# Feature projections on half rows of the matrix engine in one burst, four banks read in two orders, and a last output group in two halves

## The chip, the cores and the metric

The kernel runs on one core of a Trainium2 chip. The core has five engines that run side by side, each through its own list of instructions: TensorE (PE in the profile; its weight loads are listed apart as PEld), VectorE (DVE), ScalarE (ACT), GpSimd (POOL) and SyncE (SP, which here only issues transfers). Matmuls write to PSUM, which the kernel uses as eight banks of 128 partitions by 512 fp32 values. The metric is the device time in microseconds (us). Differences below 0.2% are about what a measurement of this kernel can't tell from no change.

## What is computed

Two stages, for batch 8, 8 heads, 576 tokens, head size 64:

```python
def phi(x):                                   # q and k, (8, 8, 576, 64) -> (8, 8, 576, 256)
    proj = einsum('bhsd,df->bhsf', x, w_phi)  # 128 features
    proj = proj - max(abs(proj), axis=-1, keepdims=True)
    return concatenate([exp(proj), exp(-proj)], axis=-1)
kv  = einsum('bhsf,bhsd->bhfd', phi(k), v)
num = einsum('bhsf,bhfd->bhsd', phi(q), kv)
den = einsum('bhsf,bhf->bhs', phi(q), sum(phi(k), axis=2)) + 1e-06
x   = num / den                               # then heads side by side: (8, 576, 512)

h = relu(x @ w_in)                            # (8, 576, 1024)
u, v = h[..., :512], h[..., 512:]
v = (v - mean(v)) / sqrt(var(v) + 1e-06)
v = einsum('ts,bsd->btd', w_spatial, v) + b_spatial[None, :, None]
out = (u * v) @ w_out                         # (8, 576, 512), fp32
```

Note the subtraction of the largest absolute projection. For keys the kernel takes the exponentials without it and scales the values by the exponential of the maximum; for queries it adds the negated maximum inside the matmul that makes the features.

## The kernel before

**Units.** The attention is cut into 36 units. A pair unit is two heads of one batch on 512 of its 576 tokens (four blocks of 128 per head); there are four for each of the eight batches. The remaining 64 tokens of two batches, all eight heads, make one tail unit, so there are four of these. A unit's keys and queries stand in SBUF as `kT` and `qT`: 128 partitions, of which the lower 64 hold the 64 dimensions of one block of tokens and the upper 64 those of another, times four column groups of 128 tokens.

**Projection by token.** `by_token` (L263 to L268) makes half a unit's projections: two matmuls with a column group of `kT` or `qT` as the weights and `wphi2` as the moving operand. `wphi2` is 128 by 256 and block diagonal: `w_phi` in the upper left, `w_phi` in the lower right, zeros elsewhere. So half of the products of each matmul are with zeros. One PSUM bank takes the two results, four blocks of 128 features.

**Readers of the banks.** `a_keys` (L270) does two halves, each: two matmuls, then the maximum on VectorE (`mk`, L278), then two exponentials on ScalarE (`kf`, L281). `a_queries` (L283) does two halves of matmuls and maxima only (`mq`, L292), and then `mhl` splits the maxima into two bf16 parts (L295, L296; GpSimd, or VectorE in the first five units). `a_scale` (L298) makes `em` on ScalarE from `mk`, and GpSimd scales the values with it into `vs` (L306).

**Order of the work.** `step(i)` writes the instructions of one step by hand, in the order of the list `ORDER` (L622). Each entry names a piece of work for a unit, some steps behind by `LAGS`, followed by a share of filler: `fill` pops tasks of the second stage from a queue while a credit lasts. The tasks of a batch come to 16.7 us by the costs that the kernel gives them (`MM` = 0.85 us and `MS` = 1.07 us), over 4.5 units, so a step has about 3.7 us of filler. The tasks are `b_v` (v half of w_in, L447, evicted by ScalarE at L449, statistics on VectorE at L450), `b_u` (L515, L517), `b_s` (spatial matmul L536 and L537, product on VectorE at L539), and `b_o` (output, L561, evicted by VectorE and ScalarE in turn at L564, sent off by SyncE at L570) with their 64-token tails.

**The other pieces of a step.** `sums` is `a_kv` (L378, L380), `attention` is `a_num` (L398, then L388 and L389 on VectorE), `features` is `a_qfeat` (L344, exponentials at L365), `maxima` is `a_max_t` (L327, then L330 and L331 on VectorE), `next` is `a_transpose`, which from batch 2 on has nothing to do for pair units since they are transposed by transfers.

**PSUM.** All PSUM tiles come from one pool of eight banks (`psum`, tag `bank`). A matmul that takes a bank anew waits until all readers of the bank's last tile are done.

**The end.** `out_tasks` (L598) of the last batch are four `b_o` and then `b_o_tail` (L572), which evicts 128 rows and sends them as two transfers of 64 rows each.

Of the kernel before, what the change touches and what calls it, by code (L numbers as in the profile page):

```python
# [8 lines left out]
FP32 = mybir.dt.float32  # L9
BF16 = mybir.dt.bfloat16  # L10
AF = mybir.ActivationFunctionType
ALU = mybir.AluOpType
AX = mybir.AxisListType
# [3 lines left out]
def kernel(  # L17
# [15 lines left out]
    nc = tc.nc  # L33

    B, H, S, D = q.shape
    F = w_phi.shape[1]
    DM = moe_w_in.shape[0]
    DFF = moe_w_in.shape[1]
    HALF = DFF // 2
    P = 128  # L40
    KC = DM // P
    NP = H // 2
    NB = 4
# [3 lines left out]
    POS = [0, 2, 1, 3]  # L47
# [5 lines left out]
    feat = ctx.enter_context(tc.tile_pool(name="feat", bufs=2))  # L53
    small = ctx.enter_context(tc.tile_pool(name="small", bufs=3))
    s2 = ctx.enter_context(tc.tile_pool(name="stage_b", bufs=2))

    psum = ctx.enter_context(tc.tile_pool(name="psum", bufs=8, space=bass.MemoryType.PSUM))
# [13 lines left out]
    st = {}  # L71
# [67 lines left out]
    bias = cpool.tile([P, NB], FP32)  # L139
# [8 lines left out]
    wphi2 = cpool.tile([P, 2 * F], BF16)  # L148
# [10 lines left out]
    NM = 3  # L159
    mhl, mT = [], []  # L160
    for i in range(NM):
        for tiles, name in ((mhl, "mhl"), (mT, "mT")):
            t = cpool.tile([P, P], BF16, name=f"{name}{i}")
# [21 lines left out]
    for y in range(2):  # L185
        r = slice(y * D, (y + 1) * D)
# [7 lines left out]
    for i in range(2):  # L194
        pin(nc.scalar.copy)(out=alternate(wm, i),
                            in_=wphi2[:, i * F:(i + 1) * F].unsqueeze(1).to_broadcast([P, NP, F]))
# [20 lines left out]
    w_out_bf = cpool.tile([P, KC, DM], BF16)  # L217
# [7 lines left out]
    EARLY = 5  # L225
# [22 lines left out]
    def a_transpose(u):  # L248
        if u["pair"] and u["b"] >= XB:
            return  # L250
        src = st[u["b"]] if u["pair"] else gs[u["g"]]
        for x, copy in (("k", nc.vector.tensor_copy if u["i"] < EK else nc.scalar.copy), ("q", nc.vector.tensor_copy)):
            pt = psum.tile([P, 4, P], BF16, tag="bank", name="pt")
            for j in range(4):
                if u["pair"]:
                    blk = src[x][u["pj"] // 2][:, 2 * (u["pj"] % 2) + j // 2, (j % 2) * P:(j % 2 + 1) * P]
                else:
                    blk = src[x][:, 2 * j:2 * j + 2, :]
                nc.tensor.transpose(out=pt[:, j, :], in_=blk, identity=ident)
            u[x + "T"] = a1.tile([P, 4, P], BF16, tag="kT", name="kT") if x == "k" else qts[u["i"] % len(qts)]  # L260
            copy(out=u[x + "T"], in_=pt)

    def by_token(xT, half):  # L263
        ps = psum.tile([P, 4, F], FP32, tag="bank", name="ps")
        for x in range(2):
            nc.tensor.matmul(out=ps[:, 2 * x:2 * x + 2, :], lhsT=xT[:, 2 * half + x, :], rhs=wphi2,  # L266
                             start=True, stop=True)
        return ps  # L268

    def a_keys(u):  # L270

        u["mk"] = small.tile([P, H], FP32, tag="mk", name="mk")
        u["kf"] = feat.tile([P, 2, H, F], BF16, tag="kf" if u["pair"] else "kf_t", name="kf",
                            bufs=4 if u["pair"] else 2)
        for half in range(2):
            pk = by_token(u["kT"], half)
            hs = slice(4 * half, 4 * half + 4)
            nc.vector.tensor_reduce(out=u["mk"][:, hs], in_=pk, axis=AX.X, op=ALU.max,  # L278
                                    apply_absolute_value=True)
            for s, sc in ((0, 1.0), (1, -1.0)):  # L280
                nc.scalar.activation(out=u["kf"][:, s, hs, :], in_=pk, func=AF.Exp, bias=0.0, scale=sc)  # L281

    def a_queries(u):  # L283

        m, early = mhl[u["i"] % NM], u["i"] < EARLY
        if not early:
            mq = small.tile([P, H], FP32, tag="mq", name="mq")
        for half in range(2):
            pq = by_token(u["qT"], half)
            if early and half == 0:  # L290
                mq = pq[:, 0, 0:H]
            nc.vector.tensor_reduce(out=mq[:, 4 * half:4 * half + 4], in_=pq, axis=AX.X, op=ALU.max,  # L292
                                    apply_absolute_value=True)
        eng = nc.vector if early else nc.gpsimd
        eng.tensor_copy(out=m[:, 0:H], in_=mq)  # L295
        eng.tensor_tensor(out=m[:, H:2 * H], in0=mq, in1=m[:, 0:H], op=ALU.subtract)  # L296

    def a_scale(u):  # L298
        em = small.tile([P, 2, H], FP32, tag="em" if u["pair"] else "em_t", name="em", bufs=3 if u["pair"] else 1)
# [25 lines left out]
    def a_max_t(u):  # L325
        pt = psum.tile([P, P], BF16, tag="bank", name="pt")
        nc.tensor.transpose(out=pt, in_=mhl[u["i"] % NM], identity=ident)  # L327
        if merged(u):
            odd, even = u["qT"][0:2 * H], u["qE"][D:D + 2 * H]
            nc.vector.tensor_copy(out=odd, in_=pt[0:2 * H, :].unsqueeze(1).to_broadcast([2 * H, 4, P]))  # L330
            nc.vector.tensor_copy(out=even, in_=pt[0:2 * H, :].unsqueeze(1).to_broadcast([2 * H, 4, P]))  # L331
            return
        nc.vector.tensor_copy(out=mT[u["i"] % NM][0:2 * H, :], in_=pt[0:2 * H, :])
# [224 lines left out]
    def o_mm(lhs, r):  # L558
        po = psum.tile([P, DM], FP32, tag="bank", name="po")
        for dc in range(KC):  # L560
            nc.tensor.matmul(out=po[r], lhsT=lhs(dc), rhs=w_out_bf[:, dc, :], start=(dc == 0), stop=(dc == KC - 1))  # L561
        ob = s2.tile([P, DM], FP32, tag="ob", name="ob", bufs=6)
        turn[0] ^= 1
        (nc.vector.tensor_copy if turn[0] else nc.scalar.copy)(out=ob[r], in_=po[r])  # L564
        return ob

    def b_o(b, j):
        ob = o_mm(lambda dc: st[b]["uT"][:, dc, j * P:(j + 1) * P], slice(0, P))
        dst = bass.AP(tensor=out.tensor, offset=out.offset + b * S * DM + POS[j] * DM, ap=[[NB * DM, P], [1, DM]])
        nc.sync.dma_start(out=dst, in_=ob)  # L570

    def b_o_tail(g, bls):  # L572
        r = slice(bls[0] * TL, (bls[-1] + 1) * TL)
        ob = o_mm(lambda dc: gs[g]["uTt"][:, dc, r], r)
        for bl in bls:
            nc.sync.dma_start(out=out[2 * g + bl, T0:S, :], in_=ob[bl * TL:(bl + 1) * TL, :])
# [18 lines left out]
    MM = KC * T0 / 2400.0  # L595
    MS = (KC + 1) * T0 / 2400.0

    def out_tasks(b):  # L598
        ts = [(MM, lambda j=j: b_o(b, j)) for j in range(NB)]
        if b % 2:  # L600
            ts.append((MM, lambda: b_o_tail(b // 2, [0, 1])))
        return ts

    def b_tasks(b):
# [11 lines left out]
        for y in range(NB):  # L616
# [2 lines left out]
        ts.append((MS / 2, lambda: b_s_tail(g, [bl])))  # L619
        return ts + (out_tasks(b) if b == B - 1 else [])  # L620

    ORDER = (("keys", 0.375), ("queries", 0.25), ("attention", 0), ("sums", 0.25),  # L622
             ("next", 0.125), ("features", 0), ("out", 0), ("maxima", 0))
    MOST = 4.0
    rate = [MOST]
    CAP = 2.11
# [5 lines left out]
    def fill(share):  # L632
        credit[0] = min(credit[0] + rate[0] * share, CAP)
        while queue and credit[0] >= queue[0][0] / 2:
            cost, task = queue.pop(0)
            task()
            credit[0] -= cost
# [3 lines left out]
    def lag(u, what):  # L641
        if u["i"] < 5:
            return (HEAD if u["i"] < 2 else FIRST if u["pair"] else FT).get(what, 0)
        return LAGS.get(what, 0)
# [3 lines left out]
    def step(i):  # L648

        if i == 0:  # L650
            a_transpose(units[0])
        left = [p - i + 1 for p in lists if p >= i]
        rate[0] = min(MOST, sum(cost for cost, _ in queue) / left[0]) if left else MOST
        for what, share in ORDER:
            for u in units[max(0, i - 5):i + 2]:
                if u["i"] + lag(u, what) != i or (what in ("sums", "attention", "out") and not u["pair"]):
                    continue
                last = u["pair"] and u["pj"] == NP - 1
                if what == "keys":
                    a_keys(u)  # L660
                    a_scale(u)
                elif what == "sums":
                    a_kv(u)
                elif what == "queries":
                    a_queries(u)
                elif what == "next":
                    a_transpose(u)
                elif what == "maxima":
                    a_max_t(u)
                elif what == "out":  # L670
                    a_x_t(u)
                    if last:
                        finish_batch(u, tail_x_t)
                        queue.extend(b_tasks(u["b"]))
                elif what == "features":
                    a_qfeat(u)
                elif what == "attention":
                    a_num(u)
                    if last:
                        finish_batch(u, tail_num)  # L680
            fill(share)

    def finish_batch(u, f):
        f(u["g"], [u["b"] % 2])
# [34 lines left out]
    for u in units:  # L719
        i = u["i"]  # L720
# [48 lines left out]
```

## Time and profile before

| | |
|---|---|
| time, median of 3 runs | 278.79 us (278.53 to 278.94) |
| span of the profiled execution | 275.7 us |
| POOL busy | 184.4 us, 67% of the span |
| PEld busy | 171.3 us, 62% |
| granted TensorE clock | full in all 40 slices |
| L281, `kf`, ACT | 144 instructions, 638 ns each, 75.4 us busy |
| L365, `qf`, ACT | 128 instructions, 625 ns each, 66.6 us busy |
| L278, `mk`, DVE | 72 instructions, 681 ns each, 46.3 us busy |
| L292, `mq`, DVE | 62 and 10 instructions, 678 and 690 ns each, 46.8 us busy |
| L266, `ps`, PE | 288 matmuls of 256 columns, 272 to 296 ns each by kind |

The duration of a single instruction includes a tail in which the next one of the same engine already runs: neighbouring matmuls of 256 columns have 273 ns each but start 109 ns apart. So for an engine's rate, starts are read, or the length of a merged run of instructions. Busy time counts overlapping stretches once. The clock is full all the time, so no difference in what follows comes from it.

### The profile page before, as it was taken

The numbers are of one execution on the slowest core, as the hardware profiler recorded it, in microseconds if no ns is written. First come the engines' busy times: TensorE is split into PE (matmuls) and PEld (weight loads), VectorE is DVE, ScalarE is ACT, GpSimd is POOL, SyncE is SP. The second block draws the span as 40 slices with busy tenths as digits, with TensorE's granted clock in tenths as the row PEclk, the third lists the DMA queues.
The fourth block names the chain that finished last, engine by engine and source line by source line (L and its number), as shares of the span: only waits on it lengthen the run. The fifth ranks groups of instructions, "written<-read, shape, count | busy, mean of one in ns | idle before, by whom it ended". The sixth has DMA issues, their size and how long they took to land.

```text
span 275.7 us, 8138 instructions
## 1 busy us (share of the span) xinstructions
PE 254.7 (92%) x3007; PEld 171.3 (62%) x3047; DVE 236.5 (86%) x614; ACT 218.1 (79%) x501; POOL 184.4 (67%) x312
## 2 busy tenths in 40 slices
PE   3778999999999999999998999999998999999993
PEld 2467776777665766666665775766655765554441
DVE  7989999879999889998889899988898897565751
ACT  7898999797698978999798979998798977633511
POOL 7999899999569945897787954997347632410200
PEclk9999999999999999999999999999999999999999
DMA  7999999999999997999999998899744301211115
GB/s 209 230 228 146 164 155 113 181 208 122 202 200 219 232 212 133 232 176 199 156 110 221 258 183 146 171 233 176 104 89 118 88 2 73 81 40 40 76 40 190
DMA packets 84840, 42.43 MB, mean 154 GB/s; under 512 B 51840, under 2 KB 80192, under 8 KB 84800
## 3 DMA queue, kind: packets, MB, share of 16 engines
q1 hardware_dynamic: 60240, 30.95, 54.5%
q0 software_dynamic: 24400, 10.89, 38.5%
q8 instruction: 24, 0.39, 0.6%
q14 instruction: 16, 0.13, 0.2%
q10 hardware_dynamic: 160, 0.07, 0.1%
HBM read 32.85 MB, written 9.44 MB: 153 GB/s over the span
## 4 chain that ended last, share of the span: by engine, by line
PE 70%; ACT 14%; DVE 11%; issue 3%; ACTq 0%; DVEq 0%
PE pv L447 10%; PE ps L536 10%; PE po L561 9%; PE pu L515 8%; PE ps L266 7%; ACT kf L281 7%; PE pv L378 4%; PE pn L398 4%; ACT qf L365 4%; DVE mk L278 3%; PE pq L344 3%; PE ps L537 2%; PE pn L426 2%; ACT vr L449 1%; PE pu L527 1%
## 5 line engine op out<-in xcount | busy, mean ns | idle before, releaser
L306 POOL TENSOR_TENSOR vs<-v_f,em 128x512 bf16<-128x512 f32 x64 | 65.4, 1042 | 27.8 <-ACT em L301 25.3
L281 ACT ACTIVATE kf<-ps 128x512 bf16<-128x512 f32 x144 | 75.4, 638 | 6.5 <-DVE mk L278 6.5
L365 ACT ACTIVATE qf<-pq 128x512 bf16<-128x512 f32 x128 | 66.6, 625 | 9.6 <-PE pq L344 7.5
L278 DVE TENSOR_REDUCE mk<-ps 128x4 f32<-128x512 f32 x72 | 46.3, 681 | 0.7
L292 DVE TENSOR_REDUCE mq<-ps 128x4 f32<-128x512 f32 x62 | 39.9, 678 | 2.2 <-PE ps L266 2.0
L561 PE MATMUL po<-w_out_bf,uT 128*128 128x512 bf16 x120 | 31.9, 379 | 1.4 <-ACT kf L281 0.8
L461 POOL TENSOR_TENSOR rs<-var,neghalf 64x1 f32<-64x1 f32 (+1 forms) x16 | 12.8, 797 | 30.5 <-DVE var L456 30.3
L536 PE MATMUL ps<-w_spT,vn 128*128 128x512 bf16 x119 | 32.5, 379 | 0.5
L450 DVE BATCH_NORM_STATS2 stats<-vr 128x6 f32<-128x512 bf16 (+1 forms) x40 | 26.7, 684 | 6.5 <-ACT vr L449 6.2
L447 PE MATMUL pv<-w_in_bf,xT 128*128 128x512 bf16 x117 | 30.7, 379 | 1.2 <-ACT kf L281 0.6
L515 PE MATMUL pu<-xT,w_in_bf 128*128 128x512 bf16 x119 | 31.1, 379 | 0.5 <-issue 0.2
L449 ACT ACTIVATE vr<-pv 128x512 bf16<-128x512 f32 (+1 forms) x40 | 23.8, 620 | 8.9 <-PE pv L447 8.1
L539 DVE TENSOR_TENSOR uT<-ps,uT 128x512 bf16<-128x512 f32 x32 | 22.0, 687 | 8.5 <-PE ps L537 7.6
L378 PE MATMUL pv<-vs,kf 128*128 128x66 bf16 x512 | 24.5, 193 | 1.3 <-ACT kf L281 1.1
L389 DVE TENSOR_TENSOR x<-pn,rc 128x256 bf16<-128x256 f32 x64 | 25.0, 416 | 0.3
L398 PEld LDWEIGHTS <-qf 128*128 128x128 bf16 x512 | 20.2, 97 | 7.4 <-issue 1.7
L517 ACT ACTIVATE uT<-pu 128x512 bf16<-128x512 f32 x32 | 19.7, 643 | 6.3 <-PE pu L515 3.2
L378 PEld LDWEIGHTS <-kf 128*128 128x128 bf16 x512 | 21.7, 97 | 3.6 <-issue 2.9
L398 PE MATMUL pn<-kv,qf 128*128 128x66 bf16 x512 | 21.9, 193 | 0.9 <-ACT kf L281 0.3
L380 PE MATMUL pv<-vst,kf 128*128 128x66 bf16 x128 | 21.2, 192 | 1.4 <-POOL vst L61 1.4
L564 ACT COPY ob<-po 128x512 f32<-128x512 f32 x18 | 11.0, 613 | 14.3 <-PE po L561 8.8
L467 POOL TENSOR_SCALAR vn<-vr,rs 128x512 bf16<-128x512 bf16 x28 | 21.2, 764 | 0.9
(130 smaller groups left out, 562.6 us busy)
## 6 DMA issues: line engine op xcount, KB each, us to landing
out_dram<-ob SPq DMA_DIRECT2D x32, 256.0 KB, 2.7
v_f<-in_v_dram SPq DMA_DIRECT2D x14, 512.0 KB, 5.6
k_bf<-in_k_dram POOLq DMA_DIRECT2D x14, 256.0 KB, 6.3
q_bf<-in_q_dram POOLq DMA_DIRECT2D x14, 256.0 KB, 5.9
qt<-qT_b SPq DMA_DIRECT2D x24, 64.0 KB, 4.2
v_tl<-in_v_dram SPq DMA_DIRECT2D x8, 128.0 KB, 5.9
v_f<-in_v_dram SPq DMA_DIRECT2D x1, 1024.0 KB, 8.8
w_in_bf<-in_moe_w_in_dram POOLq DMA_DIRECT2D x2, 512.0 KB, 7.0
```

The costliest lines, as they stand in the source:

```text
L278: nc.vector.tensor_reduce(out=u["mk"][:, hs], in_=pk, axis=AX.X, op=ALU.max, apply_absolute_value=True)
L281: nc.scalar.activation(out=u["kf"][:, s, hs, :], in_=pk, func=AF.Exp, bias=0.0, scale=sc)
L292: nc.vector.tensor_reduce(out=mq[:, 4 * half:4 * half + 4], in_=pq, axis=AX.X, op=ALU.max, apply_absolute_value=True)
L306: nc.gpsimd.tensor_tensor(out=vs[:, s, :, 0:D], in0=st[u["b"]]["v"][:, pj * H:(pj + 1) * H, :], in1=em[:, s, :].unsqueeze(2).to_broadcast( ...
L365: nc.scalar.activation(out=qf[:, s], in_=pq, func=AF.Exp, bias=0.0, scale=sc)
L378: nc.tensor.matmul(out=pv[:, hh, s, :], lhsT=u["kf"][:, s, 4 * hh + c, :], rhs=u["vs"][:, s, 4 * hh + c, :], start=(c == 0), stop=False)
L398: nc.tensor.matmul(out=pn[:, pos, :], lhsT=u["qf"][hh][:, s, pos, :], rhs=d["kv"][:, 2 * u["pj"] + hh, s, :], start=(s == 0), stop=(s == 1))
L447: nc.tensor.matmul(out=pv[r], lhsT=lhs(kc), rhs=w_in_bf[:, kc, HALF:DFF], start=(kc == 0), stop=(kc == KC - 1))
L450: nc.vector.bn_stats(out=stats[r], in_=dst[r])
L515: nc.tensor.matmul(out=pu, lhsT=w_in_bf[:, kc, dc * P:(dc + 1) * P], rhs=d["xT"][:, kc, :], start=(kc == 0), stop=(kc == KC - 1))
L536: nc.tensor.matmul(out=ps, lhsT=d["vn"][:, sp, cs], rhs=w_spT[:, sp, 0:T0], start=(sp == 0), stop=False)
L561: nc.tensor.matmul(out=po[r], lhsT=lhs(dc), rhs=w_out_bf[:, dc, :], start=(dc == 0), stop=(dc == KC - 1))
```

## The change

Three edits:

1. `by_token` makes the projections of a whole `kT` or `qT` with eight matmuls of 128 columns that use 64 rows each: block `j` of the lower half with the upper left `w_phi`, into bank 0, then block `j` of the upper half with the lower right `w_phi`, into bank 1. `a_project` does so for keys and queries, one after the other, so four banks are filled in one burst of 16 matmuls.
2. `a_readers` writes the reads. VectorE takes key bank 0, query bank 0, key bank 1, query bank 1. ScalarE takes key bank 1 and then key bank 0. So the first reads of the two engines are of different banks. The places of the results are interleaved to match (`parity`, and the rearranged `hi` and `lo` of `mhl`), and `mhl` now stands ahead of `vs` on GpSimd. `ORDER` loses the entry `queries`; its share of filler, 0.25, goes to the end of the step, behind `maxima`.
3. The last batch's output has its tail as the second of five groups, and the last group of 128 rows is done by `b_o_last` as two halves of 256 columns, one evicted by ScalarE and sent from ScalarE's queue, one evicted by VectorE and sent from SyncE's.

The purpose is to leave out the products with zeros, to let two engines read at once, and to shorten what follows the last matmul.

```diff
-    def by_token(xT, half):
-        ps = psum.tile([P, 4, F], FP32, tag="bank", name="ps")
-        for x in range(2):
-            nc.tensor.matmul(out=ps[:, 2 * x:2 * x + 2, :], lhsT=xT[:, 2 * half + x, :], rhs=wphi2,
-                             start=True, stop=True)
+    def by_token(xT):
+        ps = [psum.tile([P, 4, F], FP32, tag="bank", name="ps") for _ in range(2)]
+        for j in range(4):
+            for y in range(2):
+                r = slice(y * D, (y + 1) * D)
+                nc.tensor.matmul(out=ps[y][:, j, :], lhsT=xT[r, j, :], rhs=wphi2[r, y * F:(y + 1) * F],
+                                 start=True, stop=True)
         return ps
...
+    def a_project(u):
+        u["pk"], u["pq"] = by_token(u["kT"]), by_token(u["qT"])
...
+        def features(y):
             for s, sc in ((0, 1.0), (1, -1.0)):
-                nc.scalar.activation(out=u["kf"][:, s, hs, :], in_=pk, func=AF.Exp, bias=0.0, scale=sc)
...
+                nc.scalar.activation(out=kf[:, s].rearrange("p (j two) f -> p j two f", two=2)[:, :, y, :],
+                                     in_=u["pk"][y], func=AF.Exp, bias=0.0, scale=sc)
+
+        most(parity(mk, 0), u["pk"][0])
+        features(1)
+        most(mq[:, 0:4], u["pq"][0])
+        features(0)
+        most(parity(mk, 1), u["pk"][1])
+        most(mq[:, 4:8], u["pq"][1])
         eng = nc.vector if early else nc.gpsimd
...
+    def b_o_last(b, j):
...
+        for y, copy, queue_ in ((0, nc.scalar.copy, nc.scalar), (1, nc.vector.tensor_copy, nc.sync)):
+            n = slice(y * DM // 2, (y + 1) * DM // 2)
+            po = psum.tile([P, DM // 2], FP32, tag="bank", name="po")
+            for dc in range(KC):
+                nc.tensor.matmul(out=po, lhsT=st[b]["uT"][:, dc, j * P:(j + 1) * P], rhs=w_out_bf[:, dc, n],
+                                 start=(dc == 0), stop=(dc == KC - 1))
+            ob = s2.tile([P, DM], FP32, tag="ob", name="ob", bufs=6)
+            copy(out=ob[:, 0:DM // 2], in_=po)
+            queue_.dma_start(out=dst[:, n], in_=ob[:, 0:DM // 2])
...
+        if b == B - 1:
+            ts = ts[:1] + ts[-1:] + ts[1:NB - 1] + [(MM, lambda: b_o_last(b, NB - 1))]
...
-    ORDER = (("keys", 0.375), ("queries", 0.25), ("attention", 0), ("sums", 0.25),
-             ("next", 0.125), ("features", 0), ("out", 0), ("maxima", 0))
+    ORDER = (("keys", 0.375), ("attention", 0), ("sums", 0.25),
+             ("next", 0.125), ("features", 0), ("out", 0), ("maxima", 0.25))
...
                 if what == "keys":
-                    a_keys(u)
+                    a_project(u)
+                    a_readers(u)
                     a_scale(u)
```

More of the change, by code (lines that the diff above doesn't have):

```diff
@@ L261, in a_transpose @@
             copy(out=u[x + "T"], in_=pt)
-    def by_token(xT, half):
-        ps = psum.tile([P, 4, F], FP32, tag="bank", name="ps")
-        for x in range(2):
-            nc.tensor.matmul(out=ps[:, 2 * x:2 * x + 2, :], lhsT=xT[:, 2 * half + x, :], rhs=wphi2,
-                             start=True, stop=True)
-        return ps
[L270 to L279, printed above, removed]
-            for s, sc in ((0, 1.0), (1, -1.0)):
-                nc.scalar.activation(out=u["kf"][:, s, hs, :], in_=pk, func=AF.Exp, bias=0.0, scale=sc)
@@ L283, in a_queries @@
[L283 to L293, printed above, removed]
+    def by_token(xT):
[5 more added lines that the diff above has]
+                                 start=True, stop=True)
+        return ps
@@ new lines, in parity, with a_readers, most @@
+    def parity(t, y):
+        return t.rearrange("p (j two) -> p j two", two=2)[:, :, y]
+    def a_project(u):
+        u["pk"], u["pq"] = by_token(u["kT"]), by_token(u["qT"])
+    def a_readers(u):
+        m, early = mhl[u["i"] % NM], u["i"] < EARLY
+        u["mk"] = mk = small.tile([P, H], FP32, tag="mk", name="mk")
+        u["kf"] = kf = feat.tile([P, 2, H, F], BF16, tag="kf" if u["pair"] else "kf_t", name="kf",
+                                 bufs=4 if u["pair"] else 2)
+        if early:
+            mq = u["pq"][0][:, 0, 0:H]
+        else:
+            mq = small.tile([P, H], FP32, tag="mq", name="mq")
+        def most(out, ps):
+            nc.vector.tensor_reduce(out=out, in_=ps, axis=AX.X, op=ALU.max, apply_absolute_value=True)
+        def features(y):
+            for s, sc in ((0, 1.0), (1, -1.0)):
+                nc.scalar.activation(out=kf[:, s].rearrange("p (j two) f -> p j two f", two=2)[:, :, y, :],
[6 more added lines that the diff above has]
+        most(mq[:, 4:8], u["pq"][1])
@@ L294, in a_queries @@
         eng = nc.vector if early else nc.gpsimd
-        eng.tensor_copy(out=m[:, 0:H], in_=mq)
-        eng.tensor_tensor(out=m[:, H:2 * H], in0=mq, in1=m[:, 0:H], op=ALU.subtract)
+        hi, lo = (m[:, e * H:(e + 1) * H].rearrange("p (j two) -> p two j", two=2) for e in range(2))
+        mq = mq.rearrange("p (two j) -> p two j", two=2)
+        eng.tensor_copy(out=hi, in_=mq)
+        eng.tensor_tensor(out=lo, in0=mq, in1=hi, op=ALU.subtract)
     def a_scale(u):
@@ L570, in b_o @@
         nc.sync.dma_start(out=dst, in_=ob)
+    def b_o_last(b, j):
+        dst = bass.AP(tensor=out.tensor, offset=out.offset + b * S * DM + POS[j] * DM, ap=[[NB * DM, P], [1, DM]])
+        for y, copy, queue_ in ((0, nc.scalar.copy, nc.scalar), (1, nc.vector.tensor_copy, nc.sync)):
[7 more added lines that the diff above has]
+            queue_.dma_start(out=dst[:, n], in_=ob[:, 0:DM // 2])
     def b_o_tail(g, bls):
@@ L663, in step @@
                     a_kv(u)
-                elif what == "queries":
-                    a_queries(u)
                 elif what == "next":
```

## The prediction

> **What bounds the kernel now.** I read the page's busy times first, then its chain, then busy time by stretch, then single steps in order of time.
>
> ```profile
> PE 254.7 (92%) x3007; PEld 171.3 (62%) x3047; DVE 236.5 (86%) x614; ACT 218.1 (79%) x501; POOL 184.4 (67%) x312
> ...
> PE 70%; ACT 14%; DVE 11%; issue 3%; ACTq 0%; DVEq 0%
> ```
>
> The shares say that TensorE is fullest and holds most of the chain that ended last, but they average over a ramp, a middle and an end. So by stretch:
>
> ```profile
> 0.00:20.00 20.00, 12.10 (x118) 8.75 (x119) 17.86 (x50) 16.82 (x39) 17.62 (x29) 1.00 1.03 228
> ...
> 100.00:140.00 40.00, 39.58 (x474) 26.74 (x480) 37.09 (x92) 35.64 (x84) 29.14 (x52) 1.00 1.07 175
> 140.00:180.00 40.00, 38.84 (x475) 26.36 (x480) 37.54 (x99) 35.73 (x85) 29.50 (x50) 1.00 1.18 186
> 180.00:220.00 40.00, 37.84 (x464) 25.89 (x470) 35.27 (x88) 34.69 (x82) 27.12 (x50) 1.00 0.75 134
> ```
>
> The columns after the width are PE, PEld, DVE, ACT, POOL. In the ramp VectorE and ScalarE set the pace. From about 60 us to 225 us PE does, at 38.7 of 40 on average, but DVE follows at 36.5 and ACT at 35.0. After 225 us there are no projections left, and PE runs alone. This small distance between three engines is what the forecast hangs on: a saving on PE can be taken up for about 2 us in 40 and no further.
>
> **What the skill says.** The Trainium skill, "TensorE: Matmul & The Clock Gate", section "Part 3: Packing small matmuls", has it that matmuls on different row groups run concurrently, their starts some 4 ns apart. No matmul of the kernel before is paired so; the trace can't say. "TensorEngine Tiling (Array Packing)", section "Key Properties", says that a change of tiling mode drains TensorE. The trace has that, with a price:
>
> ```profile
> 104.74 0.28 PE L344 MATMUL pq<-qT_b,wm 128*128 128x128 bf16 x2
> 104.95 0.29 PE L439 MATMUL pt<-ident,xt 64*128 64x64 bf16 x4
> 105.17 0.23 PE L327 MATMUL pt<-ident,mhl 128*128 128x128 bf16 x1
> 105.23 0.60 PE L266 MATMUL ps<-wphi,kT 128*128 128x256 bf16 x4
> ```
>
> The L344 pair lasts 0.28 and one of them 0.22, so the second starts at 104.80. Its successor would follow 0.056 later, since L344's four groups of two stand 0.11 apart, but the 64-row L439 starts at 104.95: 0.09 for entering the mode. The last of the four L439 (0.193 each) starts at 105.05, and L327 at 105.17 where 0.03 would do: 0.09 for leaving. "PSUM — Partial Sum Buffer", section "PSUM bank collisions raise a hardware error", says that two engines must not use one bank at once, reads included, so they are kept apart by waits. The trace agrees:
>
> ```profile
> ACT kf L281 <- DVE mk L278: 6.5, 13, 0.8
> ...
> DVE stats L450 <- ACT vr L449: 6.2, 10, 1.7
> ```
>
> **The change part by part.**
>
> *The burst.* Now: 8 matmuls, 109 ns from start to start (four L266 last 0.60, one 0.273, so 0.33 for three steps), 0.87 us a unit. After: 16 of 128 columns in 64-row mode. If pairs overlap, 8 times 56 ns = 0.45, plus 0.19 for mode in and out = 0.64: 0.235 saved. If they don't, 16 times 56 ns plus 0.19 = 1.09: 0.22 lost. The 16 weight loads, twice the former, don't bind: in L548 and L550 (five matmuls of 64 columns, each with its own load) starts are 29 ns apart, and 16 of these are 0.47. I take the overlap, as the page states it and the two row groups write to two banks. Units whose burst lies in PE's stretch: numbers 11 to 35, the bursts from 60 to 221 us, 25 of them. Freed: 25 times 0.235 = 5.9 us.
>
> How much of this shows? In 40 us there are some 6 bursts, so PE falls by 1.4, to 37.3, with DVE unchanged at 36.5, since it has the same reductions of the same size. Engines that wait on each other in order don't run closer than that without loss, and I let half through: 2.9 us.
>
> *The orders of reading.* ScalarE no longer waits for the first maximum. That wait was 6.5 us in 13 places, of which 1.6 us in 4 lie before 40 us, where ACT and DVE are the chain. I take half of these 1.6, 0.8 us, as DVE bounds the ramp just as well; those after 60 us are on an engine with slack and count nothing. The new wait is VectorE's: its third read, key bank 1, must follow ScalarE's two exponentials. Behind it in the queue stand the last maximum, the normalisation of attention (L388, L389) and the statistics (L450). PE waits for these only a step or more later, GpSimd for `mhl` and `em` at once, but it is busy 29.8 of 40. A step shows how close this is:
>
> ```profile
> 139.52 1.09 ACT L365 ACTIVATE qf<-pq 128x512 bf16<-128x512 f32 x2
> ...
> 140.11 0.69 DVE L278 TENSOR_REDUCE mk<-ps 128x4 f32<-128x512 f32 x1
> ...
> 140.95 2.12 ACT L281 ACTIVATE kf<-ps 128x512 bf16<-128x512 f32 x4
> ```
>
> ScalarE was still at the features when VectorE began. With two exponentials at 1.1 and two reductions at 1.2, VectorE would have waited 0.84 + 1.1 - 1.2 = 0.74 here. But the filler moved behind `maxima`, about 0.9 us of matmuls, lets ScalarE finish the features before the burst; most of the 0.74 goes. I cost it at nothing in the likeliest case, hidden by the reductions' own 1.2 us, and keep 0 to 0.74 a unit for the range.
>
> *Four banks at once.* PE already stops once for a bank that ScalarE holds:
>
> ```profile
> 150.01 1.02 PE L561 MATMUL po<-w_out_bf,uT 128*128 128x512 bf16 x3 [0.75 <-ACT kf L281]
> ```
>
> Key bank 0 is now ScalarE's last, free some 2.1 us after it starts, while PE needs a ninth bank after about 2 us: filler, 0.375 of 3.7 = 1.4 us, and attention, 16 matmuls at 31 ns = 0.5. Bounds 0 and 0.75 a unit; I take nearly 0, being part of the half that I don't let through.
>
> *mhl ahead of vs* on GpSimd: nothing, `em` is ready no earlier than the last maximum (after four exponentials, 2.1 us, against four reductions, 2.4).
>
> *The end.*
>
> ```profile
> 271.27 0.58 ACT L564 COPY ob<-po 128x512 f32<-128x512 f32 x1 [1.14 <-PE po L561]
> 271.88 1.11 SPq L576 DMA_DIRECT2D out_dram<-ob  x2
> ```
>
> Two issues take 1.11 us, so the second starts about 0.5 after the first, at 272.4, and lands 2.3 later (the median in this stretch) at 274.7; the span ends 1.0 after that. In the change the last half is evicted by VectorE in 0.42 (L389, 128x256) instead of 0.58, from the same 271.27, and its single transfer is issued at 271.7 and lands at 274.0. PE's work is the same (eight times 109 ns for four times 216). The other half is 0.4 earlier, on another queue. Tail rows go out behind two groups of matmuls. 0.7 us saved.
>
> Sum: 2.9 + 0.8 + 0.7 = 4.4, so 278.8 - 4.4 = 274.4.
>
> **Rivals.**
>
> *All of it shows* (0.26). DVE and ACT turn out to have more room than their busy shares tell, since part of their idle time is waiting for PE (L539 waits 7.6 us for PE, L449 8.1, L365 7.5). 5.9 + 1.6 + 0.7 = 8.2: 270.6. For it: these waits. Against: DVE's 36.5 of 40.
>
> *New waits take the place of the saving* (0.15). VectorE behind ScalarE on key bank 1, or PE behind ScalarE on a bank. With 0.4 us a unit, about half of either bound, 25 times (0.4 - 0.235) = 4.1, less 0.7 at the end: 282.2, slower. For it: the two steps above. Against: the moved filler.
>
> *No overlap of row pairs* (0.09). 25 times 0.22 = 5.5 lost, 1.5 won elsewhere: 282.8, slower. Only the page speaks against it.
>
> *A draw* (0.08). The waits eat just what the burst and the ramp give, within a few tenths: 278.5.
>
> **How the numbers follow.** The likeliest, 0.42, gives 274.4. Faster: 0.42 + 0.26 + 0.02 of the draw = 0.70. Same: 0.06, the rest of the draw. Slower: 0.15 + 0.09 = 0.24. For the range, the low end is a microsecond below the full saving, 269.5, for steps that gain on other waits too. The high end, 282.0, takes in the draw and waits up to 0.39 a unit. It leaves out about 0.15 above and 0.05 below.
>
> **What would show it.** A burst of 16 matmuls 0.45 us from first to last start, with 0.09 ahead and behind (else the third rival). PE's busy time in the middle down and DVE's share up towards 38 of 40. In the list of waits, `kf` on `mk` gone; if in its place `mk` on `kf` stands at more than 5 us, or PE on `kf`, the second rival is at work. The last landing 0.7 us closer to PE's end. The prediction is wrong if the middle is no shorter though the burst is.

## The result, and the profile after

275.07 us (median of 4 runs, 274.37 to 276.04) against 278.87 (278.53 to 279.31) beside it; the ratio is 0.9865, interval 0.9829 to 0.9902. In two later comparisons the same kernel gave 0.9858 (0.9825 to 0.989) and 0.9898 (0.987 to 0.9926). Five of the changed kernel's 24 executions took 278.5 to 281.4 us, while none of the 145 of the kernel before stood so far above its fastest; the ratios leave such long executions out, the medians in the table of the experiments don't, and with them counted the means are 276.5 and 278.6 us.

The page of the changed kernel, in the same two places as before:

```profile
PE 252.5 (92%) x3339; PEld 161.8 (59%) x3339; DVE 236.8 (87%) x615; ACT 219.0 (80%) x501; POOL 182.2 (67%) x312
...
PE 64%; ACT 14%; DVE 13%; DMA 4%; issue 2%; POOL 1%; SPq 0%; DVEq 0%
```

PE has 292 more weight loads (288 from the bursts, 4 from the last group) and yet 2 us less busy time; DVE and ACT have nearly the same. (PE's own count rises by 332, since some 40 matmuls are missing from the records before.) By stretch:

```profile
0.00:20.00 20.00, 10.56 (x124) 7.47 (x125) 16.43 (x46) 15.78 (x35) 15.75 (x28) 1.00 1.06 226
...
100.00:140.00 40.00, 39.88 (x547) 24.88 (x545) 37.73 (x92) 35.71 (x83) 30.94 (x54) 1.00 1.27 188
140.00:180.00 40.00, 38.69 (x531) 24.30 (x530) 38.26 (x102) 36.31 (x86) 29.92 (x53) 1.00 1.18 173
180.00:220.00 40.00, 39.03 (x528) 24.11 (x526) 36.61 (x90) 36.47 (x86) 26.34 (x47) 1.00 0.89 153
```

VectorE and ScalarE do more in each of these 40 us than before, since the same work passes faster, and DVE stands at 37.5 of 40 on average. In the first 20 us every engine does less than before (DVE 16.4 instead of 17.9): the ramp has become slower. One burst in the middle, TensorE in order of time:

```profile
132.91 0.38 PE L547 MATMUL ps<-w_spT,vnt 128*128 128x512 bf16 x1
133.22 0.40 PE L268 MATMUL ps<-wphi,kT_b 64*128 64x128 bf16 x8
133.46 0.39 PE L268 MATMUL ps<-wphi,qT_b 64*128 64x128 bf16 x8
133.78 0.39 PE L546 MATMUL ps<-w_spT,vn 128*128 128x512 bf16 x1
```

From 133.22, eight matmuls are done within 0.40, the last 0.22 of which is one matmul's own length. So the eighth starts 0.18 after the first, where seven steps of 0.056 would take 0.39: row pairs run together, the two of a pair 3 ns apart in the trace. L547 starts at 132.91 and would be followed after 0.22; the burst starts after 0.31: 0.09 for the entry. From the burst's start to the next work there are 0.56 us, of which 0.09 are the exit. In all 0.65 us a unit. The reads of these banks, first ScalarE's list and then VectorE's:

```profile
131.65 2.06 ACT L375 ACTIVATE qf<-pq 128x512 bf16<-128x512 f32 x4 [0.64 <-PE pq L354]
133.69 2.07 ACT L293 ACTIVATE kf<-ps 128x512 bf16<-128x512 f32 x4
136.19 0.31 ACT L311 ACTIVATE em<-mk 128x8 f32<-128x8 f32 x2 [0.43 <-DVE mk L289]
```

```profile
133.94 0.68 DVE L289 TENSOR_REDUCE mk<-ps 128x4 f32<-128x512 f32 x1
134.54 0.68 DVE L289 TENSOR_REDUCE mq<-ps 128x4 f32<-128x512 f32 x1
135.13 0.68 DVE L289 TENSOR_REDUCE mk<-ps 128x4 f32<-128x512 f32 x1
```

ScalarE comes out of the features just as the burst is done and starts before VectorE. The waits between the two, in the middle (45 to 222 us):

```profile
DVE mk L289 <- ACT kf L293: 2.4, 6, 1.0
...
ACT kf L293 <- DVE mk L289: 1.1, 3, 0.4
```

Before, in this stretch:

```profile
ACT kf L281 <- DVE mk L278: 4.3, 8, 0.8
```

And the end:

```profile
269.05 0.37 ACT L591 COPY ob<-po 128x256 f32<-128x256 f32 x1 [0.71 <-PE po L588]
269.44 0.42 DVE L591 COPY ob<-po 128x256 f32<-128x256 f32 x1 [0.18 <-PE po L588]
269.45 0.36 ACTq L592 DMA_DIRECT2D out_dram<-ob  x1
269.90 0.42 SPq L592 DMA_DIRECT2D out_dram<-ob  x1
```

The last transfer is issued 0.46 us after VectorE's start, where before the second one went out 1.13 us after ScalarE's (271.27 to 272.40).

### The profile page after: what moved, and what is told of

It reads as the page before. It is cut to its first block, busy times and chain, and to the rows that moved or that the text cites. A ratio compares the mean times of both kernels' runs of the same rounds, so it can differ in the third digit from the quotient of the medians.

```text
span 273.7 us, 8737 instructions
## 1 busy us (share of the span) xinstructions
PE 252.5 (92%) x3339; PEld 161.8 (59%) x3339; DVE 236.8 (87%) x615; ACT 219.0 (80%) x501; POOL 182.2 (67%) x312
## 4 chain that ended last, share of the span: by engine, by line
PE 64%; ACT 14%; DVE 13%; DMA 4%; issue 2%; POOL 1%; SPq 0%; DVEq 0%
PE ps L546 10%; PE pv L457 9%; PE po L571 9%; PE pu L525 8%; ACT qf L375 6%; ACT kf L293 6%; PE ps L268 4%; PE pv L388 3%; PE pn L408 3%; DVE mk L289 3%; PE pq L354 3%; DVE stats L460 3%; DMA q_bf<-in_q_dram 2%; PE ps L547 2%; DVE mq L289 2%
## 5 line engine op out<-in xcount | busy, mean ns | idle before, releaser
L293 ACT ACTIVATE kf<-ps 128x512 bf16<-128x512 f32 x144 | 76.8, 647 | 3.0 <-PE ps L268 1.7
L289 DVE TENSOR_REDUCE mk<-ps 128x4 f32<-128x512 f32 x72 | 49.2, 683 | 7.7 <-ACT kf L293 4.1
L289 DVE TENSOR_REDUCE mq<-ps 128x4 f32<-128x512 f32 x62 | 41.3, 677 | 0.0
L525 PE MATMUL pu<-xT,w_in_bf 128*128 128x512 bf16 x128 | 32.2, 379 | 1.9 <-DVE mq L289 0.9
L546 PE MATMUL ps<-w_spT,vn 128*128 128x512 bf16 x128 | 33.1, 380 | 0.0
L457 PE MATMUL pv<-w_in_bf,xT 128*128 128x512 bf16 x128 | 31.8, 379 | 0.6 <-ACT kf L293 0.2
L460 DVE BATCH_NORM_STATS2 stats<-vr 128x6 f32<-128x512 bf16 (+1 forms) x40 | 27.3, 686 | 5.3 <-ACT vr L459 4.8
L459 ACT ACTIVATE vr<-pv 128x512 bf16<-128x512 f32 (+1 forms) x40 | 24.9, 630 | 7.8 <-PE pv L457 7.4
L574 ACT COPY ob<-po 128x512 f32<-128x512 f32 x17 | 10.4, 614 | 13.5 <-PE po L571 8.1
```

The costliest lines, as they stand in the source:

```text
L289: nc.vector.tensor_reduce(out=out, in_=ps, axis=AX.X, op=ALU.max, apply_absolute_value=True)
L293: nc.scalar.activation(out=kf[:, s].rearrange("p (j two) f -> p j two f", two=2)[:, :, y, :], in_=u["pk"][y], func=AF.Exp, bias=0.0, scale=sc)
L457: nc.tensor.matmul(out=pv[r], lhsT=lhs(kc), rhs=w_in_bf[:, kc, HALF:DFF], start=(kc == 0), stop=(kc == KC - 1))
L460: nc.vector.bn_stats(out=stats[r], in_=dst[r])
L525: nc.tensor.matmul(out=pu, lhsT=w_in_bf[:, kc, dc * P:(dc + 1) * P], rhs=d["xT"][:, kc, :], start=(kc == 0), stop=(kc == KC - 1))
L546: nc.tensor.matmul(out=ps, lhsT=d["vn"][:, sp, cs], rhs=w_spT[:, sp, 0:T0], start=(sp == 0), stop=False)
```

## The experiments

The traces allow a finer reading than the times. The start of a unit's first key maximum on VectorE marks its place in the run. The span is cut at these marks: to the sixth unit's (ramp), from the ninth unit's to the 36th's (middle, 27 units), from there to the start of the last matmul, and the rest. The three units between the sixth mark and the ninth, 14.6 to 14.9 us in every kernel, are left out.

Executions of one program mostly keep step once the ramp is over: in the middle the first two of the changed kernel differ by 0.7 us, nearly all of it at the twelfth unit, and the two of the variant with one order in the ramp by 0.16. There is one exception: the third execution of the changed kernel that was profiled, 281.42 us in all, took 182.63 us in the middle, where 176 was expected. Why is open, and it enters no mean below.

| kernel | median us | ratio to before, interval | ramp | middle | to last matmul | rest |
|---|---|---|---|---|---|---|
| before | 278.87 | 1 | 26.05 | 180.15 | 49.76 | 4.94 |
| changed | 275.07 | 0.9865 (0.9829 to 0.9902) | 28.96 | 175.54 | 49.99 | 4.56 |
| changed, again | 275.21 | 0.9858 (0.9825 to 0.989) | 29.34 | 176.25 | 49.99 | 4.55 |
| end alone | 278.86 | 1.0003 (0.9987 to 1.002) | 27.30 | 180.14 | 49.85 | 4.51 |
| full rows | 278.58 | 1.0 (0.9979 to 1.0021) | 28.90 | 178.64 | 50.22 | 4.58 |
| one order | 277.47 | 0.9937 (0.9916 to 0.9957) | 26.44 | 179.04 | 49.92 | 4.55 |
| full rows, one order | 279.45 | 1.003 (1.0012 to 1.0048) | 27.29 | 181.57 | 50.15 | 4.52 |
| pairs in the old order | 279.23 | 1.0025 (1.0008 to 1.0042) | 27.39 | 181.13 | 49.77 | 4.54 |
| filler behind burst | 278.74 | 1.0012 (0.9997 to 1.0028) | 28.31 | 174.71 | 54.50 | 4.51 |
| filler behind attention | 280.33 | 1.0068 (1.0041 to 1.0095) | 28.18 | 180.50 | 50.80 | 4.54 |
| same, one order in the ramp | 279.74 | 1.0048 (1.0029 to 1.0067) | 28.23 | 180.57 | 50.80 | 4.54 |
| changed, third time | 275.83 | 0.9898 (0.987 to 0.9926) | 27.61 | 182.63 | 49.99 | 4.56 |
| one order in the ramp | 273.65 | 0.983 (0.9802 to 0.9858) | 26.32 | 176.00 | 49.99 | 4.53 |
| the last, again | 275.21 | 0.9823 (0.9771 to 0.9875) | 27.77 | 176.16 | 49.99 | 4.52 |

The theory to be tested was that of the prediction (A): pairs give most of the gain in PE's stretch, the end gives 0.7, the orders matter little. The rival (B): burst and orders give it, and pairs are immaterial. After the first four of these runs, A became A2: pairs and orders each give a part, and the parts add up. Each variant has one profile, unless the table says otherwise.

**The changed kernel again, and the end alone.** The second has the third edit only, everything else as before.

> The changed kernel once more, beside the variants. Both theories: 275.1 us, between 274.3 and 276.1. If its first 25 us again take about 3 us longer up to the sixth unit's first key maximum (28.96 against 26.05 before) with the matrix clock at half there, the loss in the ramp belongs to the change; if the sixth unit comes at about 26, it was a late load in that one execution.

> The kernel before with only the third edit (tail output second, last group in two halves). Theory A (paired half rows in TensorE's stretch give most of the gain, the end 0.7 us): 278.1, that is 0.7 us below before. Rival B (the burst and the orders of reading give it, pairing is immaterial): also 0.7 below. Rival C (the end gives most of it): 275.1.

The ramp of the changed kernel is long in both executions (28.96, 29.34). But the old program is not at 26.05 each time either: with the end alone, where the first 220 us are the old program, the sixth unit came at 27.30. The difference starts with a load. GpSimd before and with the end alone:

```profile
5.64 0.61 POOL L61 CAST k_bf<-first 128x512 bf16<-128x512 f32 x1 [0.71 <-DMA first<-in_k_dram]
```

```profile
6.32 0.61 POOL L61 CAST k_bf<-first 128x512 bf16<-128x512 f32 x1 [2.23 <-DMA first<-in_k_dram]
```

The same load of the keys landed 0.7 us later, and GpSimd issues later loads behind its cast. The first three units' marks are the same to 0.02 us; the fourth comes at 18.35 instead of 16.25, after TensorE has waited for such a load:

```profile
15.39 0.34 PEld L259 LDWEIGHTS <-q_bf 128*128 128x128 bf16 x4 [1.25 <-DMA q_bf<-in_q_dram]
```

Before, this wait was 0.39. TensorE also ran at half its clock here from 14.78 to 18.19 us. Against this ramp, 27.3, the changed kernel's two are about 2 us longer. As to the end, the time shows no gain that can be told from none; the trace shows 4.94 to 4.51, that is 0.4 us, less 0.1 ahead of the last matmul. The 0.3 that remain lie inside the interval.

**The square of pairs and orders.** Three kernels. *Full rows*:

```diff
-                r = slice(y * D, (y + 1) * D)
-                nc.tensor.matmul(out=ps[y][:, j, :], lhsT=xT[r, j, :], rhs=wphi2[r, y * F:(y + 1) * F],
+                nc.tensor.matmul(out=ps[y][:, j, :], lhsT=xT[:, j, :], rhs=wphi2[:, y * F:(y + 1) * F],
```

*One order*:

```diff
         most(parity(mk, 0), u["pk"][0])
-        features(1)
-        most(mq[:, 0:4], u["pq"][0])
         features(0)
         most(parity(mk, 1), u["pk"][1])
+        features(1)
+        most(mq[:, 0:4], u["pq"][0])
         most(mq[:, 4:8], u["pq"][1])
```

The third has both edits.

> The changed kernel, but each of the 16 matmuls of the burst uses all 128 rows, half of them zeros in the weight matrix, so no pairs and no change of mode: 16 times 56 ns = 0.90 us a burst instead of 0.65 with the mode's cost. Orders, banks and the end stay as changed. Theory A: 25 bursts lose 0.25 us each, 6 us, of which half to all shows: 278 to 281. Rival B: no more than 0.5 us above the changed kernel, 275.1 to 275.6.

> The changed kernel with both engines reading key bank 0 first: VectorE takes key 0, key 1, query 0, query 1, ScalarE key 0, key 1. ScalarE then waits for VectorE's first maximum again. Theory A: the orders matter little, 274.8 to 275.8. Rival B: ScalarE's wait of up to 0.65 us a unit comes back in 36 units, half of it on the path of the ramp and the middle: 277 or more.

> All 128 rows in the burst's matmuls and both engines on key bank 0 first: burst and place of the filler alone. Fills the square of pairs by orders. If pairs and orders add up (theory A2), from the ninth unit's first maximum to the last unit's it takes 181.7 us (176 changed, plus 2.7 for full rows, plus 3 for one order); if each works only with the other (theory E, with one order VectorE and ScalarE bind and TensorE's time doesn't matter), no more than 179.5.

In the middle, two orders: 176.0 with pairs (mean of 175.54, 176.25, 176.00 and 176.16) against 178.64 without, so pairs give 2.6. One order: 179.04 against 181.57, 2.5. And the orders give 3.0 with pairs and 2.9 without. In the middle the two add up: 181.57 against the 181.7 that additivity gave. In the whole time, where the ramp has its part, the ratios (0.9858 for the changed kernel) fit less well: pairs 4.0 and 2.6 us, orders 2.2 and 0.8. So each theory had half of it: B is wrong that pairs are immaterial, A that the orders are. With one order, in the middle:

```profile
ACT kf L293 <- DVE mk L289: 9.9, 14, 1.3
```

ScalarE waits for the first maximum 9.9 us in 14 places, where with two orders both directions of waiting come to 2.4 + 1.1 us. TensorE pays for it: its own waits that ScalarE ended come to 4.2 us in 11 places, against 1.5 in 5 with two orders. Its longest single wait there is for a transfer, 1.3 us, where executions with two orders have 0.6 or none:

```profile
PE ps L268 <- DMA qT_b<-q_bf: 1.3, 1, 1.3
PE pu L525 <- ACT kf L293: 1.0, 2, 0.8
PE pn L436 <- ACT kf L293: 0.8, 2, 0.4
```

The edit changes VectorE's order and ScalarE's together; which of them does it, no run separates. Full rows and one order together take 1.4 us longer than the kernel before (181.57 against 180.15): the burst and what comes with it (the moved filler, the interleaved results, `mhl` ahead of `vs`) are a loss without pairs and orders. Up to 0.5 of the 1.4 are the matmuls themselves, by their starts 0.89 us a unit where the old ones took 0.87.

**Pairs in the old order.** The sequence of `ORDER` of before with keys and queries apart, both engines on key bank 0 first, matmuls in pairs, the new end. The interleaved results stay.

> Paired half rows in the order of before: keys, filler, queries, filler, both engines on key bank 0 first; the new end. Two bursts a unit, so two entries and exits of the mode: 0.45 + 0.38 = 0.83 us of TensorE instead of 0.87. Theory A2: within 0.5 us of before less the end's 0.4, 277.8 to 278.7. Rival B' (what counts is that keys' two banks come at once): 277 or less.

Slower than expected: 1.0 us more in the middle than before, though by the starts the bursts take 0.85 us a unit instead of 0.87. That pairs are worth 2.6 us in one burst and nothing in two is in line with two mode changes more a unit; why it is a loss at all, no run tells.

**Where the filler stands.** First with 0.625 behind the burst and 0 behind the maxima, then with the quarter behind attention:

```diff
-    ORDER = (("keys", 0.375), ("attention", 0), ("sums", 0.25),
-             ("next", 0.125), ("features", 0), ("out", 0), ("maxima", 0.25))
+    ORDER = (("keys", 0.375), ("attention", 0.25), ("sums", 0.25),
+             ("next", 0.125), ("features", 0), ("out", 0), ("maxima", 0))
```

> The changed kernel with the last quarter of the filler moved from behind the maxima to behind the burst (shares 0.625, 0.25, 0.125, 0). ScalarE then has the features' exponentials still ahead of it when the burst comes, and VectorE waits for it at key bank 1, 0.74 us in the step that the prediction took. If the place of the filler is what hides that wait: 25 times up to 0.74, some 5 us or more above the changed kernel, 278 to 281. If not: 275 to 276.

> The changed kernel with the last quarter of the filler behind attention, where the shares come in the sequence of before (0.375, 0.25, 0.25, 0.125) and the cap of the credit takes no more than it did there; with 0.625 behind the burst it cut filler off the middle and left 4.5 us of it for the end. If the place behind the maxima hides VectorE's wait for ScalarE: ninth to last unit takes 178 us or more (176 as changed), total 277 or more. If the place is of no account: 175.5 to 176.5 and 275.2.

The first doesn't answer the question. The credit has a cap (`CAP`, 2.11), a share of 0.625 at a rate of up to 4 runs into it, and filler was lost to the end: the middle is 1.3 us shorter, but the stretch behind the last unit, where PE runs alone, is 4.5 longer. The second keeps the filler in the middle, and costs 4.5 us there (180.50) and 0.8 behind it. So, with pairs and two orders, the place behind the maxima is worth more than either of them, but not by the wait that was supposed. In the middle of that variant VectorE's waits are

```profile
DVE qT_b L340 <- PE pt L337: 5.4, 6, 1.7
...
DVE mk L289 <- ACT kf L293: 2.2, 5, 1.0
```

The wait at key bank 1 is the same 2.2 as with the filler behind the maxima (2.4). What has grown is the wait for the maxima's transpose on TensorE, from 1.9 to 5.4 us, and TensorE's own waits for VectorE, from 1.9 to 6.0. The longest of these are now:

```profile
PE pn L408 <- DVE qt L341: 1.4, 2, 0.8
PE po L571 <- DVE mq L289: 1.4, 2, 0.9
```

My reading is that filler between the maxima and the burst gives VectorE and ScalarE time to hand over before four banks are claimed at once; no run isolates it.

**One order in the ramp.** The changed kernel with the reads of "one order" where `u["i"] < 8`.

> The changed kernel, but the first eight units read with both engines on key bank 0 first, as in the variant with one order; from the ninth on the two orders differ. In the traces the changed kernel is about 2 us behind at the sixth unit (28.96 and 29.34 us against 26.44 with one order, 27.30 in the old program with equally late loads) and gains 3 us on the one-order variant after that. Theory A2 (the ramp's loss is the orders of reading, and is independent of the middle's gain): 273.2, 2 us below the changed kernel. Rival D (the lost time is idle time that the middle takes up anyway, behind loads): 275.2, as the changed kernel.

> As the one before, with one order of reading in the first eight units. Additive: 1.6 us below it, as between the changed kernel and the variant with one order in the ramp.

> One order of reading in the first eight units, two from then on, once more, on the same chip as the changed kernel: 273.2 to 274, 1.5 to 2 us below it. If the ramp was only lucky the first time, as the changed kernel.

> The changed kernel once more, beside the variants on one chip: 275.2, and again about 176 us from the ninth unit to the last.

The first time the median is 1.6 us below the changed kernel as it was repeated (273.65, 275.21), with a middle as short. The second time, both on one chip, the ratios are 0.9823 and 0.9898, which is 2 us; the intervals just touch (0.9875 and 0.987). That is the size that was expected. In the traces the sixth unit is at 26.32 and 27.77. Over all profiles but that of 281.42 us, the five with two orders in the ramp have it at 28.2 to 29.3, 28.7 in the mean, and the six of edited kernels with one order there at 26.3 to 28.2, 27.2 in the mean. One profile proves little in the ramp; the ratios carry it: this version is the fastest that was run. With the filler behind attention the ramps are the same in one profile each (28.18 and 28.23), and the ratios differ by 0.6 us with intervals that overlap, where I expected 1.6.

VectorE's list shows what the two orders do in the ramp. With one order:

```profile
7.51 0.69 DVE L289 TENSOR_REDUCE ps<-ps 128x4 f32<-128x512 f32 x1
8.11 0.41 DVE L261 COPY kT<-pt 128x512 bf16<-128x512 bf16 x1
8.44 0.69 DVE L289 TENSOR_REDUCE ps<-ps 128x4 f32<-128x512 f32 x1
```

With two, in the changed kernel:

```profile
7.89 0.69 DVE L289 TENSOR_REDUCE mk<-ps 128x4 f32<-128x512 f32 x1 [0.29 <-ACT kf L293]
8.50 0.69 DVE L289 TENSOR_REDUCE ps<-ps 128x4 f32<-128x512 f32 x1
9.10 0.42 DVE L261 COPY kT<-pt 128x512 bf16<-128x512 bf16 x1
```

(The reductions into `ps` are those of the queries, whose maxima stand in PSUM in the first units.) The next unit's `kT` is copied a microsecond later, since the copy stands behind the fourth reduction and the third has waited for ScalarE. By the next unit's first maximum the difference is 0.7 us (10.21 and 9.50). How it grows to the sixth unit is not shown, as TensorE's clock comes in. In the changed kernel:

```profile
21.32 0.42 PE L362 MATMUL pq<-mT,sel 128*128 128x128 bf16 x2
21.53 0.42 PE L358 MATMUL pq<-qt,wphi 128*128 128x256 bf16 x1
```

In the variant with one order throughout such matmuls stand 0.11 apart at 19.7 us, here 0.21, until after 23 us, and the page gives TensorE's granted clock as 0.7 in the fourth of its 40 slices. The Trainium skill, "TensorE: Matmul & The Clock Gate", section "Part 1: The HAM clock gate", has it that an idle TensorE is put on half its clock. The doubled spacing agrees; but TensorE was not idle throughout, it was busy for 1.88 of the 3.41 us before (16.69 to 20.10). And it doesn't come from the two orders. With one order in the ramp, second execution, the same matmuls are just as slow:

```profile
20.83 0.42 PE L366 MATMUL pq<-qt,wphi 128*128 128x256 bf16 x1
21.04 0.42 PE L370 MATMUL pq<-mT,sel 128*128 128x128 bf16 x2
```

Nor was the kernel before at full clock from the start, as the table of its profile has it. Its first matmuls of 256 columns are slow, too:

```profile
6.57 1.06 PE L266 MATMUL ps<-wphi,qt 128*128 128x256 bf16 x4
```

That is 1.06 us for what took 0.60 at 105.23. The page shows full clock there, as it does for the slow matmuls of the variant just shown; so in the ramp the spacing has to be read. A part of the differences there comes from the clock; how large it is, these runs don't tell.

## Why the prediction was right, and where its steps were not

The time, 275.1 for 274.4, was right, and the mechanism in the main: row pairs overlap, the middle gets shorter, the waits don't eat the gain. But the sum came out by errors against each other, and that is luck.

- **Burst, 0.87 to 0.64 us.** Right: 0.65. The pairs overlap as the page cited in the prediction states (starts some 4 ns apart, here 3), and the mode costs 0.09 on each side. "No overlap of row pairs" is out.
- **Half of 5.9 us shows, 2.9.** Right: pairs are worth 2.5 to 2.6 us of the middle. The sign given with it didn't come: from 100 to 220 us PE is busy 39.2 of 40, not 37.3 (38.8 before), and DVE 37.5, not 36.5 (36.6 before). The work passes faster, so no share falls. Why just half shows is open.
- **The waits of ScalarE after 60 us "count nothing".** The step that failed. ScalarE had slack by its busy share, but when it waits, TensorE later waits for the banks that it holds: 4.2 us of TensorE's waits are ended by ScalarE with one order, 1.5 with two. The orders were worth 2.9 to 3.0 us of the middle, as much as the pairs.
- **Four banks at once "nearly 0", and the moved filler only as a cover.** Mis-sized both ways: the burst with what comes along costs 1.4 without pairs and orders, and the place of the filler is worth 4.5 with them, by another wait than the one I named.
- **Ramp, 0.8 gained.** Wrong in sign. By the ratios with and without two orders there, these cost 1.6 to 2 us; against the kernel before about 0.8 are lost, as the sum below has it. I counted the wait that goes (`kf` on `mk`) and not the one that comes (the third reduction on ScalarE), nor that the next unit's copy is queued behind it. I had asked what stands behind the waiting instruction in the middle, and not in the ramp.
- **End, 0.7.** 0.4. The last issue went out 0.8 earlier against the last matmul, as reckoned, but the landing took longer: 2.9 us for the last transfer and 3.1 for ScalarE's beside it, where the prediction used 2.3. Three others were still under way when the last was issued; that they are the reason is not shown.

The middle won 4.2 us (180.15 to 175.9) instead of 2.9: 2.6 of the pairs and 3.0 of the orders, less 1.4. The end won 0.4 instead of 0.7, the units between ramp and middle won 0.2, and the stretch up to the last matmul lost 0.2. The ramp lost 2.5 in the traces (29.15, the mean of two executions, against 26.7, of two of the old program) instead of winning 0.8. That makes 2.1 in all, where the medians differ by 3.8. The remainder is the choice of executions: the two profiled ones of the old program took 277.5 and 278.5 us, 0.9 below their medians in the mean, and those of the changed kernel 275.5 and 276.5, 0.9 above. If all of this lies in the ramp, as most differences between executions do, a usual execution loses about 0.8 us there.

## What to carry to other kernels

Where two engines read a set of banks in turn, try letting them start on different banks, even where one of them has idle time: here the time saved was not that engine's but TensorE's, which waits for the banks. But look at the start of the kernel on its own, where the new wait can cost more than the old one, and use the old order there if it was the better. And move one piece at a time: of the things in this one edit two won about 3 us each in the middle, the burst that came with them lost, and the place of the filler was worth more than any.

## What was not expected of the hardware

From the twelfth unit's mark to the 36th's two executions of the changed kernel take 156.46 and 156.42 us, with four engines busy, and the two with one order in the ramp 156.46 and 156.43; yet a third of the changed kernel took 163.21. Otherwise, what makes single times scatter by 2 us comes about in the ramp. There one load that landed 0.7 us late (5.6 against 6.3) was followed by a sixth unit 1.2 us late, with TensorE's matmuls 0.21 instead of 0.11 us apart for 3.4 us in between. In the changed kernel the clock was halved after a stretch of 3.41 us in which TensorE had been busy for 1.88, more than half of the time.
